# First quad of an attention kernel loaded, transposed and copied one head of each pair at a time, with a rewritten instruction order

## Chip, cores, metric

One core of a Trainium2 chip. The metric is the device time of one execution in microseconds, as the median of several runs; lower is better. In the profile PE is TensorE, PEld its weight load, DVE VectorE, ACT ScalarE, POOL GpSimd and SP SyncE.

## What is computed

Thresholded attention over 8 batches of 8 heads, 576 positions and head size 64, all in float32, followed by a feed-forward layer with a maximum over three projections:

```python
scores = scale * np.matmul(q, k.transpose(0, 1, 3, 2))
thresh = np.max(scores, axis=-1, keepdims=True) - tau          # tau = 0.02
scores = np.where(scores >= thresh, scores, -1000000000.0)
attn = np.exp(scores - max); attn = attn / (sum + 1e-09)
x = (attn @ v) as [4608, 512]
h = np.maximum(np.maximum(x @ w1, x @ w2), x @ w3)              # [4608, 768]
out = h @ w_out                                                # [4608, 512]
```

## The kernel before

Four heads of a batch make a quad; there are 16. A quad holds two pairs of heads; in the code r is the pair and i the head within it. q and k of a quad lie in tiles `qm` and `km` of 128 partitions: head i of each pair is in partitions 64i to 64i + 63, and the two pairs lie beside each other in a partition, each as nine row blocks of 64 numbers. In `transposed`, TensorE turns them with float32 transposes of 64 partitions, head by head, into a PSUM bank (`tp`); `evacuated` copies the bank into `qt` (on ScalarE, which also scales) or `kt` (on VectorE). Of `qt` there is a second copy, `qs`, whose upper and lower 64 partitions are exchanged (`swapped`), so that both row halves of TensorE can work on a score tile at once.

Work goes on in chunks of 128 query rows; a quad has nine, and a chunk has two halves r, one for each pair. Each of the 288 chunk halves runs through one score bank S (`scores`), a maximum m on VectorE, exponents e on ScalarE, and numerators with their sum. The mask list `MASKED` says for each chunk half which way is taken: a 1 lets VectorE apply the threshold after an exponential (letter k, `scalar_tensor_tensor`), a 0 lets ScalarE do it with two activation passes (letter n). After that come a reciprocal r, the normalised bf16 tile P on GpSimd (letter p), a transposing DMA t into `ptq`, the product with v (O, `product`), and the FFN of a whole batch (F and B: the two row halves of a `ph` or `po` piece; h, v, u evacuate them). Letter T is a transposition of a later quad, with a and c for its evacuation and q for its `qs` copies. Letters l and g are loads of q, k, v and of weights, y and z their casts on GpSimd, and o a store.

Nothing is scheduled at run time. The string `ORDER` is read letter by letter, and each letter issues one step; a digit after S, T, O or F names one of four PSUM slots of two banks each. The wrapper `_Ordered` keeps the written order on each engine, so each engine works through its instructions in this order and waits where data is missing. Everything of quad 0 is issued before the string begins: twelve warming transposes on TensorE, `load(0, first=True)`, four `transposed` pieces with their evacuations, and the swapped copies. In this first quad only, VectorE makes one half of each `qs` copy and ScalarE the second `kt`. All instructions go through the wrapper, so the profile puts nearly all of them on its line, L89; tiles tell them apart. DMA transfers use eight completion semaphores in turn, in the order of the program, so a transfer waits until the one eight places ahead of it has landed.

Batch 7 is processed in two parts (`SPLIT`), the last of which leaves only a short FFN at the very end.

Of the kernel before, what the change touches and what calls it, by code (L numbers as in the profile page):

```python
# [23 lines left out]
MASKED = """  # L24
101000100110000110011100001010010001100010001000101000010000100000100010
000011110101100001001001001001000001011100101011000110001010010000010011
001010011101100000101100100001001010000110011111000001000100000110000101
001001001101100000110001000100101000001100010011100101110110000001111111
"""
# [8 lines left out]
ORDER = """  # L38
glllllS0lylS1mylyeS2zmlkS3lelmnlT0mS1aS2rmeqS0meqmeS3pnkT1pT0nrcaptemS0yeS1mgS2eympeS3mqtnT1S0mqnS2knrceprmS
1epkepeS3mnyS0rkptemnS2pmnlzmS3erremtpT0empS1eklpaS2kgnS0ptnmeprrmlS1epS3mleS2pmlS0eplmetpmeS1knS3tkernkS2pt  # L40
nmnprmtepmS1eqS0melpmT2ntrmT3pnrcpatekS3pekS2eqnrS1mtnqmS0pemepS3tmeqS2kepT1lnrcnprtmS0nT1pmS3epmgS2atpmeO1k
yermeO0knptrerT3wpnT2wcS1aptmnS3pS2xmptS1emzS0emeS3zgmeS2lrmpnS0lmO1eplmeplknO3qlnrwleplwkS1xqgS2ertmF3npF0m
eT1pBrteBkyhS2cpnS3mpS1nvF2npmF0eqBmeqBrrvepS3tkhT2pS1nmS0lapmetS2pmeS3mzeF0mF1ezgBrnF2vpgnBktByeF0rvhpS3ntS
2pmF1npmBeBqrveT3zncT0F2taqvS3nBpmnS0tprhS1rmpeS3mtpS2emeyS0mteF1zmeF3kBelqBnvgF2pngT0vBnqlrS1cphS3lrmnS0plm
O2eplmeptS1ewpS3nmF0znmS2lBezkgO3etymyS1vegkF0ntF2wnrrmpBxBpveS3phS0mtnF1prmeBprS2evptS3nmF0pnS1mplBermS3ztn
S2vnzS1meS0tmpeF3mperkS2petBmepmS0tkuF1ukelkT3elBkntrarmpS2uS3pmulS0eymtO1empnrO2kpewS3xpwS1elmpF2lmF0eyqBrl
keT3ytBhcF1pnT2vT3qlaBclnS0qvlS2nqtF3mnyF1meS0pBemBthrrF2kpeS3vnBpmF0nS1pveBrprS3mhtS2pmeS0pmeS1tpmF2emF3peB
tkeT0BvaF1onvqT2T0tBcqaS3nkqS0lhrmS2nlpmF1elpF3meBlkBelF0vntS2rvnBpS1mhplS3melF0mS2teBrmepS1rkpO3emnqO2tnrvp
nwyS0xlprwS3emoF2pmoT1eyBpctS3evyF0nS1mtnS2pmBeympF1hkS3eyF2rekT0ptBamBnpS0veF3qtvS1urmnpS2mF3epketT0nkT1Bnr
mparrcpS2uS1pumtS0empS3emqoS1eF2mqlemqleS3kplnS0mBlepmlekT1teO3kunktO0urcpnrrwlS2nplS1wxmpS3lmpS0eompS1eF2mt  # L50
peF3meBkBetS0khF1nrmF2pnBvpBerrvS3phS0mtnpS1mF2peS3mtpeBmeF1yvF0etByknBvnS2tS3rhmpS1melpS0meF3lmF2elBkeBlvT1
ntF0nvT3BacS2ohS1rrmlpnF3lmF0peoBkpeBovnT2oS1qavS3tnprO2rmpmleqS0wtnT3pS1mepO2mteqkeqF0nS1cxBywmpnS3rS2hytmS
1emF0peF3mpeBrkBpetF2vnF1pBnvS0thkS3nmF2BmeBveF0rrvpT1uS3kapS0nmS2F1pmtepmeS3rktepS0mnS2pmlBelrmeplS3kupS0lu
rmS2elpF1mnoqmeS0qreS2lmpS3elmBpelmptekO0nketO2ukurrnwpT3T1xwpcS0aF2ymyT3tpS1ceBqmS3thqF0meF2pknBtBnvF1nS3rt
rvpeBmS0phS2lmepS1lmyS3etF0meyF2mpeBkBetF1knF3vnBBrvhpS0nvT1pF2nmF3takBeS0rvplBmS1phlrS2remplF3mpleF0klBpeS1
lvnS2lpmnBtrO3mepvnptS2nwS1emF0mF3eBrkepS2hBrmS1nptvS0npT2meO3qmeycqlT0xT1wyS2lacF3ntmyT0yeF1kqBatrBrevqF0hk
S2pnoS3mF1pmBteBpveS2qntS0vpnF3mprS1mlueS3pmoS0nqmtF2epmekT1oBerocpetrkS3npS1nmS0lpumS3uopmS1eT2mF0aokeorS3r
emplS2emtpS1emBpeklqtkO3uqunO0rtmpewpT2wxtS3cpeS0mnF2tF1meBknF3lkBhlBevF2nS0vnBmS1hrrS3pmeF0pmS2eBpmteF1pveF
3kBlnS0vnlS2rrBnmlpS1hrlmpF0eF3mtpeBkpBevtS2nF1pvnT0pBtmaS3hS0metF1rmepT2BrcepS3nvptT0S2nmyS1amS3lepmS0leO2m
lelmeO1rkpewnT3pwF0xcF2nykBnS1vnBrmS3phF0rrmepS2BynmqF1levF3qlBekpF0onvS2tBqmBhqrS1lepvT2S3lampF0lmS2peoBkpe  # L60
tF1vnS3prmuS0ntqmS1eF2pmetpmeS3rkepS1tBmnpmelrS0keptS3muS1uymS0temT2yeF3pcntknT2BkelramtpS1nS2pmuS0leqrmO1tu
qrkepO3nwepmS1xpwS2metF3pmS0eqBmeF1yhrkT2pBtecF3nS0vpnlS2rmpS1nlmBpnF0lveS2tmF3eBmeBkleF1klhF2lnrBvplS0nrrvp
tBnS3mphS1myteS2mF3epmF0eBpeBtvpT1nrS2yvnlS3maF0omnqS1kBepF3temS2hpBrrmeS0ptveS1pmS3nptS2meO0pmeymnqlO3weoke
oF1wxkT0tT2S3rcapBnmlF2pnS0vqtBerrmpS1hF3mqeT2BpncF0evptF2nkBpT1nvBlaS3ylS0hmoF1yqmT2eoBqrcnF0tpS3ervT2pBmaF
1ytkqS2uvnS3qmS1epF0mepmeS2kteT3BrnrcponmpS1uryS3umtS2emF0pepomeS1opnS2mtpeO3myektnO1wnkS2xrS3rewpmS1mpBekpt
eS2muS3purmF1epF0tmeBpkS3ntBhS2rnmpO1empO3xvS2xtnkS1eF3rmpF0emByepBveF1tkS2hS3mBmF0eF2rvepBBpvS1htkO3nmO0xkS
2xeS3rmF0pF1mepBeBtvS2F3vF0mF1kBeBkhF2nrvBpnBrvpS3hS0ptmS1pmeS2mtnF0mF3eBrnpBvnF1pS2vntS0rmpBmF3phoS2eS0omeF
1tmBeBkO2vO0rvpF3kpF1uketeF3kekBwrrkpBukxpuF2F0hptF1vF2pvF0hF1tvF2rvpF0hF1vpF2vF0thF1uvF2uvF0hoF3vF1vF2hoF0v
oO3oO1wovF2xF3uoF0F1hF2vF0vF1hF2vF0vF1hF2vF0vF1hF2vF0vF1hF2vF0vF1hF2vBvF0uuooBF1uuouoo
"""  # L70
# [30 lines left out]
def kernel(  # L101
# [79 lines left out]
    def load(g, first=False):  # L181
        b, qd = quads[g]
        L = Ls[g] = dict(b=b, qd=qd, first=first)
# [516 lines left out]
```

## Time and profile before

| | |
|---|---|
| median of 3 runs | 452.37 us (450.96 to 452.71) |
| the profiled execution's own time | 451.11 us |
| its span on the core | 449.3 us |
| TensorE busy | 425.6 us (95%) |
| VectorE busy | 402.0 us (89%) |
| ScalarE busy | 392.3 us (87%) |
| GpSimd busy | 314.8 us (70%) |
| P on GpSimd | 288 instructions, mean 811 ns |
| loads of 512 KB of q (15 of them) | median 4.9 us from issue to landing |

The span is what the profiler saw from the first to the last instruction of the core; the execution's own time is 1.8 us longer. Busy time of TensorE is an upper reading, since matmuls are pipelined and their ends modelled. All lines of the profile come from this one execution, so they are compared with its 451.11 us and not with the median.

### The profile page before, as it was taken

Reading aid. Unit: us, or ns where it says so; the run is one execution under the profiler, and the core shown is the slowest. Engines: PE = TensorE matmul, PEld = TensorE weight load, DVE = VectorE, ACT = ScalarE, POOL = GpSimd, SP = SyncE. Lnnn points to the kernel's source line nnn. Section 1 sums busy time; section 2 is a strip of 40 time slices with the busy share of each in tenths; the row PEclk is TensorE's granted clock in tenths of the full one; section 3 lists DMA queues with packets and bytes.
Section 4 is the critical chain, followed back from the end, with each engine's and each line's share of the span. In section 5 each row is a group of like instructions: output and inputs, shape, how many; then the busy total and the mean of one; then the engine's idle time right before and its main releaser. Section 6 shows DMA issues by size and latency. Waiting matters only on the chain.

```text
span 449.3 us, 14063 instructions
## 1 busy us (share of the span) xinstructions
PE 425.6 (95%) x5188; PEld 314.8 (70%) x5188; DVE 402.0 (89%) x1115; ACT 392.3 (87%) x794; POOL 314.8 (70%) x416
## 2 busy tenths in 40 slices
PE   6766889999999999999999999999999999999995
PEld 6433557767688768878677867868787787787762
DVE  3999999998999999999989999999999999999541
ACT  3999999999899999999989999999999999866422
POOL 3798889989795985586776785659777787534400
PEclk8989999999999999999999999999999999999999
DMA  8989999999999999996999998999999999546622
GB/s 236 276 208 204 223 214 226 222 231 222 246 212 193 214 221 231 192 222 132 221 166 194 236 217 182 215 229 216 200 172 186 213 175 191 107 77 133 130 94 107
DMA packets 212773, 87.44 MB, mean 195 GB/s; under 512 B 185824, under 2 KB 199648, under 8 KB 212704
## 3 DMA queue, kind: packets, MB, share of 16 engines
q1 hardware_dynamic: 212144, 85.95, 93.4%
q8 instruction: 41, 0.67, 0.6%
q10 hardware_dynamic: 560, 0.59, 0.5%
q14 instruction: 28, 0.23, 0.2%
HBM read 34.60 MB, written 9.44 MB: 98 GB/s over the span
## 4 chain that ended last, share of the span: by engine, by line
PE 75%; DVE 6%; POOL 5%; DMA 5%; ACT 3%; issue 3%; SPq 1%; ACTq 0%; POOLq 0%; DVEq 0%
PE ph L89 30%; PE sc L89 26%; PE po L89 8%; PE o L89 8%; POOL P L89 3%; PE tp L89 3%; DVE z L89 3%; DVE unused L89 2%; ACT z L89 2%; DMA ptq<-P 1%; SPq L89 1%; DMA qm<-in_q_dram 1%; DMA km<-in_k_dram 1%; POOL qs L89 1%; ACT ob L89 1%
## 5 line engine op out<-in xcount | busy, mean ns | idle before, releaser
L89 POOL TENSOR_SCALAR P<-z,rs 128x576 bf16<-128x576 f32 x288 | 229.2, 811 | 89.4 <-DVE rs L89 40.6
L89 PE MATMUL sc<-kt,qs 64*128 64x256 f32 (+2 forms) x640 | 180.2, 421 | 9.2 <-ACT qt L89 3.2
L89 PE MATMUL sc<-kt,qt 64*128 64x320 f32 (+2 forms) x640 | 181.2, 432 | 4.0 <-DVE kt L89 1.2
L89 PE MATMUL ph<-xt,w 64*128 64x288 bf16 (+2 forms) x2160 | 165.0, 283 | 0.3 <-DVE hm L89 0.2
L89 PEld LDWEIGHTS <-w 64*128 64x128 bf16 (+1 forms) x2160 | 127.1, 94 | 29.4 <-issue 6.7
L89 ACT ACTIVATE z<-sc,nm 128x576 f32<-128x576 f32 x179 | 128.8, 742 | 11.6 <-DVE unused L89 9.7
L89 DVE TENSOR_SCALAR_CACHE_REDUCE unused<-sc 128x576 bf16<-128x576 f32 x179 | 130.3, 751 | 4.0 <-PE sc L89 3.4
L89 ACT ACTIVATE z<-z 128x576 f32<-128x576 f32 x179 | 121.0, 682 | 0.1
L89 PEld LDWEIGHTS sc<-kt,qs 64*128 64x128 f32 (+1 forms) x640 | 91.5, 178 | 33.3 <-ACT z L89 7.8
L89 PEld LDWEIGHTS sc<-kt,qt 64*128 64x128 f32 (+1 forms) x640 | 91.6, 177 | 21.0 <-ACT z L89 6.5
L89 DVE SCALAR_TENSOR_TENSOR z<-z 128x576 f32<-128x576 f32 x109 | 89.9, 839 | 0.3 <-ACT z L89 0.2
L89 DVE TENSOR_SCALAR_CACHE_REDUCE z<-sc 128x576 f32<-128x576 f32 x109 | 80.6, 752 | 7.4 <-PE sc L89 3.6
L89 ACT ACTIVATE z<-z,nm 128x576 f32<-128x576 f32 x109 | 81.8, 774 | 4.0 <-DVE z L89 3.4
L89 POOL COPY qs<-qt 64x640 f32<-64x640 f32 (+1 forms) x62 | 45.4, 733 | 14.7 <-ACT qt L89 11.6
L89 PE MATMUL po<-wo,hT 64*128 64x512 bf16 (+1 forms) x480 | 54.0, 356 | 0.1
L89 DVE TENSOR_TENSOR hm<-ph,hm 128x576 bf16<-128x576 f32 (+2 forms) x54 | 37.1, 687 | 12.1 <-PE ph L89 11.6
L89 ACT ACTIVATE hm<-ph 128x576 bf16<-128x576 f32 (+2 forms) x54 | 32.1, 595 | 14.9 <-PE ph L89 14.4
L89 PEld LDWEIGHTS <-hT 64*128 64x128 bf16 (+1 forms) x480 | 29.6, 97 | 16.7 <-issue 3.1
L89 DVE TENSOR_TENSOR hT<-ph,hm 128x576 bf16<-128x576 f32 (+2 forms) x54 | 37.2, 688 | 2.8
L89 PE MATMUL o<-ptq,vb 128*64 128x64 bf16 (+2 forms) x544 | 38.9, 281 | 0.2
L89 ACT ACTIVATION_READ_ACCUMULATOR z<-z 128x1 f32 x179 | 35.7, 199 | 0.0
L89 PEld LDWEIGHTS <-vb 128*64 128x64 bf16 x544 | 23.7, 111 | 14.2 <-issue 4.6
(32 smaller groups left out, 273.8 us busy)
## 6 DMA issues: line engine op xcount, KB each, us to landing
vm<-in_v_dram SPq DMA_DIRECT2D x32, 256.0 KB, 4.5
out_dram<-ob SPq DMA_DIRECT2D x32, 256.0 KB, 2.8
qm<-in_q_dram SPq DMA_DIRECT2D x15, 512.0 KB, 4.9
km<-in_k_dram SPq DMA_DIRECT2D x15, 512.0 KB, 4.7
stage<-in_moe_w_dram SPq DMA_DIRECT2D x9, 512.0 KB, 4.6
ptq<-P SPq DMA_TRANSPOSE x144, 4.1
stage<-in_moe_w_out_dram SPq DMA_DIRECT2D x3, 512.0 KB, 5.8
qm<-in_q_dram SPq DMA_DIRECT2D x16, 64.0 KB, 3.1
```

The lines of the kernel that those rows point to most:

```text
L89: ins = fn(*a, **kw)
```

## The change

The first quad is handled one head of each pair at a time. `load(0, first=True)` now issues, for i = 0 and then i = 1, loads of 64 partitions: q and k of the first head pair with nine row blocks, the tenth block (all 128 partitions, once) and the other pair. There are ten transfers of q and k instead of six; three of them are still on ScalarE's queue, and seven instead of three on SyncE's, ahead of v. Before the string begins only the i = 0 halves are transposed, evacuated and swapped; the i = 1 halves become T, a, c and q steps in the string. In all of quad 0, GpSimd makes every swapped copy, in halves of one head, and VectorE every `kt` copy. There are 14 warming transposes instead of 12, and two more after each `k` transposition (`FILL`). The three banks are used in turn (`x % 3`), because the warming one stays in use.

```diff
-WARM = 12
+WARM = 14
+FILL = (2, 2)
...
         if first:
-            for n, src, e in srcs:
-                e.dma_start(out=L[n][:, 0:8], in_=rows_of(src)[:, 0, 0:8])
-        for n, src, e in srcs:
-            e.dma_start(out=L[n][:, 8:10], in_=rows_of(src)[:, :, 8])
-            yield
-        for n, src, e in srcs:
-            if first:
-                e.dma_start(out=L[n][:, 10:18], in_=rows_of(src)[:, 1, 0:8])
...
+            for i in range(2):
+                rows = slice(64 * i, 64 * i + 64)
+                srcs = (("q", q, sync), ("k", k, sync if i else nc.scalar))
+                for n, src, e in srcs:
+                    e.dma_start(out=L[n][rows, 0:9], in_=rows_of(src)[rows, 0, 0:9])
+                if i == 0:
+                    for n, src, e in srcs:
+                        e.dma_start(out=L[n][:, 9:10], in_=rows_of(src)[:, 1, 8:9])
+                for n, src, e in srcs:
+                    e.dma_start(out=L[n][rows, 10:18], in_=rows_of(src)[rows, 1, 0:8])
...
-        elif L["first"] and r == 1:
-            scalar.activation(out=dst(L["kt"]), in_=src, func=AF.Copy)
         else:
             vector.tensor_copy(out=dst(L["kt"]), in_=src)
-    def swapped(L, r):
+    def swapped(L, r, ii=(0, 1)):
...
-        for x in range(2):
-            e = vector if x == 1 and L["first"] else pool
-            e.tensor_copy(out=L["qs"][64 * x:64 * x + 64, :, cols],
-                             in_=L["qt"][64 - 64 * x:128 - 64 * x, :, cols])
+        for x in (0, 1) if len(ii) == 2 else (1, 0):
+            pool.tensor_copy(out=L["qs"][64 * x:64 * x + 64, ii[0]:ii[-1] + 1, cols],
+                             in_=L["qt"][64 - 64 * x:128 - 64 * x, ii[0]:ii[-1] + 1, cols])
             yield
...
-        p = transposed(Ls[0], n, r)
-        p.first(x)
+        p = transposed(Ls[0], n, r, (0,))
+        p.first(x % 3)
         p.done[0]()
-        if n == "q":
-            for _ in swapped(Ls[0], r):
-                pass
+        if n == "k":
+            for _ in range(FILL[r]):
+                tensor.transpose(warm[:, 0:128], identf, identf)
+    for _ in zip(*(swapped(Ls[0], r, (0,)) for r in range(2))):
+        pass
...
-                T=((g, n, r) for g in range(1, NQ) for r in range(2) for n in "qk"),
+                T=((g, n, r) for g in range(NQ) for r in range(2) for n in "qk"),
...
-            p = transposed(Ls[g], n, r)
+            ii = (0, 1) if g else (1,)
+            p = transposed(Ls[g], n, r, ii)
```

The string `ORDER` is new throughout; each line of it differs. Its first steps were and are:

```diff
-glllllS0lylS1mylyeS2zmlkS3lelmnlT0mS1aS2rmeqS0meqmeS3pnkT1pT0nrcaptem...
+gllS0llS1mlT2lemzT3lkeS0gynlcT1amT3ayS2yecqrqT1mpS0aS3kqeS1mpeS2nmeqt...
```

In both, the first transposition of quad 1 (T0 before, the second T1 after) comes when four scores have been issued. After the last score, both strings end with the same eighteen F pieces of batch 7's first part, the last two products, and the second part's eighteen pieces; before these eighteen the old string has three FFN halves, two products, the short ninth output piece and four output halves, the new one only two output halves; it has the others ahead of its last score.

`MASKED` has 108 ones instead of 109. Counted by 36 chunk halves they were 14, 9, 13, 15, 14, 13, 12 and 19, and are 13, 9, 11, 15, 14, 13, 12 and 21.

More of the change, by code (lines that the diff above doesn't have):

```diff
@@ L24 @@
 MASKED = """
[L25 to L28, printed above, removed]
-"""
-WARM = 12
+101000100110000010011100001010010001100010001000101000010000100000101000
+000011101001100001000001001001000001011100101001100110001010010000010011
+000010110111000100101100100001001010000100111110010001000100000110000101
+001001001101100000110001000100101000001100110011100100111011001111010111
+"""
+WARM = 14
+FILL = (2, 2)
 SLOTS = 4
@@ L44 @@
[L44 to L48, printed above, removed]
@@ L69 @@
[L69 removed]
+gllS0llS1mlT2lemzT3lkeS0gynlcT1amT3ayS2yecqrqT1mpS0aS3kqeS1mpS2nmeqtqmeS0qrmnT1lpS3nclyelrmS1epmeS2mptnS3mpS
+0eT1kytekzanrmS1lempeS2mpeT3rkqtnS0cnpmS3nlqrelrmpeS1lmpnS0lmS2pelpmelpnmtS3erkpS0etmnS2pmnktS1errempT3gekpt
+ekS0nptS2amnprmS3eqmetqS1rmepT2ekpT0nS3mnpmtS1aprcnS0plmeS2lpmetyremS3qeS0mpT1gempteS2cqeS3knS1kS0nrnprmnpmT
+2tepmT3epmatrkpeS2cnS1tzmeS3rnmO0pnkqteO1meprwlnS2pwS0xmpteS1mpeS3mzelS2rknT1lS0palmeO1qtmeymnO3rlkeylnwT2pl
@@ new lines @@
+ncgS1pxrgrS2wpmetF3pnmS0S1epmBeymF0qntkF2phBeBvpF3eS0vqnBrktnpS1T2mhpamtS3ezrS2rmeS0lmpeS1mpeF2gmF3peBnyF0vn
+BkzS2eBvnS1mhF3ygymnpF0tBrerpBevtpS2nF1vpnT3mBpnT0cS2tqarmS3epS0hmtzeS1mzeS2mteF3mpnF0rktpBeBevF1qnlS2vqnBrm
+pT3ngS0cplS2hrmS3npgmO1lepmleqS2welpS0remS1pnmO3zemegkF2zxtF0wkeBnF3pgBvntBrnrvS1pS2hrmpF0mS3peBmpetF1vpeS2p
+S0nmlBnzmS3eS2rvlzeS0tmS1npmF3npmtermpS0eBmpetkeF2ektukT1uS0knBlrnmpaS3pleS0myS1ulrrukO3lynmopeO2mleqwleyS0p
+wlxS3lmpnF1tmF2qeBkpeT0tBhcF3yrT1vT0aByrcnS2tqvF1nqS0mnpS3tmeF2pmBeylBkphF0nvS1lpeBmF2tvS3eBrrmnpS0lhS1pmleS
@@ new lines @@
+2pmleS3pmtF1emF0eBketT2BrvapF3nT2vtqT1nBcpnS0rtpS2amhpS1meF0tqmF3eBrkeptBvnF2pS1nvoBynmS0hS3tmyeF1qmS2eqlBme
+S0lrnrvO3lpnkpnO1mepwteS2pwrrxS3mptnF0mT1peBcpS3elvF2nplS1mnS0lmBelrmS1eptF3mepF0knBtT1hkBarF2vpetS1vpuS3rmp
+S2tF0mepmetT1knT2BknocaS3urrS2pumoS1epmlS0emqtS2eF3mpempleS1klqeS2lmT0nBtqmekeO1knrnkpO2nrcpwS0xpwtuS1muS2pm
+eS3qtrmF1epS0meF2pomeBkBeS3lkhF0tnmF1nBrvpBerrS2vphS3mpntS0mF1peS2myetBpmnF0pvF3elBrkepBlnvS1lS2phmlS0meS3tm
+eF2mF1etBkeBvT0nF3nvT2BarcS1phS0rmpnF2mpF3teBkpeT1BvaS0nrtvS1pnmO2pnomeorS3wpeT1lS0mqntO2mqerkqelF3cxlS0nprw
@@ new lines @@
+oS1mnqBomS2eptS0mhpF1emF3pteBkyBevF2nF0vpnBkS1ythS3rmyF2pmBepBveF1trnvpS0urpT3nmS2yatS1meS0myF3eplrmepkS1ept
+S2nmS0pmBelqmelkS2elS1kuF0ourrmpS3ompeS2ompeBlmpelkeS1lkO3ulnktnO2rmpuwntqT1wT0xrpcS3aF2ymepT1BtceqS0khS1pF3
+tnmF2nqrrBmetpBvF1epS0vnpBtmS3phS2metS1mS0eF3melF2meBkBelF1knF0vBBrvhpS3nvF1pnF2mtT0kBaS3rvepBrmS0phS1meptF2
+mpeF3kBelS0vnlBmnS1orO2melprnvlqS0nlwpS1lemF3plF2rmeqtBkpeS0BhmtS1npvS3npT0mO2eymecT3xtT1wrS0acpF2emqT3tF1kq
+eBrBkapS0hS3vnF1pmtnF2ymBeyByrveS0nvpF1nmptS3uS2rpemS1pmtF0emperT3ktepS2nBmpnocqS1turS2pumS3emplT0nS1mqtaS2k
@@ new lines @@
+F3ermepmS0epS1emtBekekS2lumO0nlkelO1wnlrrulmpT0xlS3wcpeS1mqF0tF2mpeBkyeBkF3hpF1nrvBnqtS0vnBprmS2hpS3meF0ptmS
+1epBmeyF2tkeF3BvnlS1rnvpBlnS0mplS2hmF1temF3eBrkplBevF0nlT2prvS1npBtamS3phrS2mepF0tmepT1rBecpS3tnvqT2nS1mqS0a
+mpS3emS2yteO1rmeqmnlpO0wleplF1wxtkT3nF0ceBlkBnS3rvhpS2mnF1pS0rmeyBqmeF2pvF3eyBkynlBrvF1lhS0rnpoBmT2pS3vaoyS0
+mpeF1ompS2eoBkpetS3mnF0qvntS2rumS1peF0myetpmeS3knS1trmBepmeplrkS2eqoS3umlS1upmT2ntS0pmeF3metrceT0pBeklaklS1u
+qlS2umS0tqnmO3pnkleO1trrempnwpS2xwS3pmeF1pmS0etBrkepF2mhT3BnylcF1nvS3ynprlS2meBytmpS3evF0pnS2mteF1mBekBleF3r
@@ new lines @@
+khpF2tnBvS0pnrrvBlnpS1mlhS3ymelS2mtpF1emF0peBktepBT3vnS2ratvpS1nmF3pnS0moBermF1peoS2rqhBtmepS3veS0pmlS1nplS2
+mntO3mekeO1lmeoweF0twrxkT3pT2S1caBpnmF2nqS3vBeqrmtS0hpF1meT2pBncoF3qnvF2ekBtT1nrvS0paBrrmpS3hF1ymteqT2BceqS0
+nvF3pnF2kpmBuT1ptvS2aS0pmeS3qtmF1eqrmepT2oeS3cpBnktnmS0urS2rulmpS3emlpF1emptekS0pnS3mnO2mtekeO0rerwpS3wxpkS2
+pS0tBmpmelymetyS3kuS0yuF2emF1BrmepBkhyS3eS2vpnO0mtnO1kxS3xrmeS0pF1epmF2rtmBepBvepS3hS1tmnF0kF2nBkeF3mBBrvepS
+1hvpO0mO3txrS2xpeS0mpoF3mF1eBkoeBkonF0F2tvnBkF3hvBnBrvpS0rF1vpS2mptBrS3mpeS0mhptS2empF1emF3tekBBvF2okF0oBkF1
@@ L70 @@
+hkBeBvnF2vO3uvO0wrrS2xpS1mpS3mF0eptmepkF1noekS2tBmkeBukuorrF3pF2hpF0vF3pvtF2hF0pvF3rvpF2thF0vpF3vF2thF0vF3vF
+2hoF0vF3vF2hF0uvuO3oF2owvO1uoF3xF0F2hF1vF0vF2hF1vF0vF2hF1vF0vF2hF1vF0vF2hF1vF0vF2hF1vBvF0uuooBF2uuouoo
 """
@@ L182, in load @@
         b, qd = quads[g]
-        L = Ls[g] = dict(b=b, qd=qd, first=first)
+        L = Ls[g] = dict(b=b, qd=qd)
         for n in "qk":
@@ L189, in rows_of @@
             return src[b, 4 * qd:4 * qd + 4].rearrange("(r i) (p c) d -> (i p) r c d", r=2, c=9)
-        q2 = nc.scalar if first else sync
-        srcs = (("q", q, sync), ("k", k, q2))
         if first:
-            for n, src, e in srcs:
-                e.dma_start(out=L[n][:, 0:8], in_=rows_of(src)[:, 0, 0:8])
-        for n, src, e in srcs:
-            e.dma_start(out=L[n][:, 8:10], in_=rows_of(src)[:, :, 8])
-            yield
-        for n, src, e in srcs:
-            if first:
-                e.dma_start(out=L[n][:, 10:18], in_=rows_of(src)[:, 1, 0:8])
-            else:
-                e.dma_start(out=L[n].rearrange("p (r c) d -> p r c d", r=2)[:, :, 0:8], in_=rows_of(src)[:, :, 0:8])
-            yield
+            for i in range(2):
[8 more added lines that the diff above has]
+                    e.dma_start(out=L[n][rows, 10:18], in_=rows_of(src)[rows, 1, 0:8])
+        else:
+            for n, src in (("q", q), ("k", k)):
+                sync.dma_start(out=L[n][:, 8:10], in_=rows_of(src)[:, :, 8])
+                yield
+            for n, src in (("q", q), ("k", k)):
+                sync.dma_start(out=L[n].rearrange("p (r c) d -> p r c d", r=2)[:, :, 0:8], in_=rows_of(src)[:, :, 0:8])
+                yield
         L["vm"] = ld.tile([128, 4, 4, D], F32, name="vm")
@@ L255, in targets, with transposed @@
                 L["qs"] = qk.tile([128, 2, S], F32, name="qs")
-    def transposed(L, n, r):
+    def transposed(L, n, r, ii=(0, 1)):
         st = {}
@@ L266, in first @@
             for j in range(nj):
-                for i in (1, 0):
+                for i in ii[::-1]:
                     rows = slice(64 * i, 64 * i + 64)
@@ L274, in done @@
             off = 320 * r
-            evacuated(L, n, r, lambda t: t[:, :, off:off + 64 * nj],
-                      st["ps"].rearrange("p (i z) -> p i z", i=2)[:, :, 0:64 * nj])
+            evacuated(L, n, r, lambda t: t[:, ii[0]:ii[-1] + 1, off:off + 64 * nj],
+                      st["ps"].rearrange("p (i z) -> p i z", i=2)[:, ii[0]:ii[-1] + 1, 0:64 * nj])
         return _Piece((L["b"], L["qd"], n, r), first, None, [done])
@@ L645, in issue @@
         elif what in "ac":
-            p, g, r = line[what].pop(0)
+            p, g, r, ii = line[what].pop(0)
             p.done[0]()
             if what == "a":
-                line["q"].append((Ls[g], r))
+                line["q"].append((Ls[g], r, ii))
         elif what in "hvuxw":
```

27 lines of the change are left out of this document (1 added, 26 removed).

## The prediction

> **What bounds the kernel now.** I read the totals of the page first, then busy time by stretch, then the timeline and the chain of the first 15 us, which is where the change is made, and last the stretches of the end.
>
> The totals (engine, busy us, share of the span, instructions):
>
> ```profile
> PE 425.6 (95%) x5188; PEld 314.8 (70%) x5188; DVE 402.0 (89%) x1115; ACT 392.3 (87%) x794; POOL 314.8 (70%) x416
> ```
>
> Busy time by stretch. The columns are the stretch, its length, PE, PEld, DVE, ACT and POOL busy, granted clock, DMA share, GB/s:
>
> ```profile
> 10.00:20.00 10.00, 7.14 (x74) 4.73 (x71) 9.48 (x26) 8.50 (x16) 6.82 (x11) 0.93 0.95 301
> 20.00:30.00 10.00, 8.08 (x56) 4.25 (x54) 9.66 (x31) 9.98 (x23) 8.87 (x13) 0.83 0.89 184
> 30.00:40.00 10.00, 6.14 (x46) 2.88 (x44) 9.44 (x31) 9.94 (x20) 8.43 (x10) 1.00 0.99 195
> 40.00:50.00 10.00, 6.71 (x58) 3.73 (x58) 9.67 (x30) 10.00 (x22) 9.44 (x13) 1.00 1.02 216
> ```
>
> From 20 to 50 us ScalarE has nothing to spare, VectorE little, GpSimd 1 us in 10 and TensorE 2 to 4. So before the FFN has input, the softmax engines set the pace, and an earlier first score helps only if these three engines also keep their lead after it. The end is different:
>
> ```profile
> 430.00:440.00 10.00, 10.00 (x76) 6.91 (x76) 5.77 (x12) 2.63 (x6) 0.00 (x0) 1.00 0.04 11
> ```
>
> There TensorE alone runs. The start, from the timeline (start, length, instruction, idle before it):
>
> ```profile
> 5.17 0.64 PE L89 MATMUL tp<-identf,qm 64*128 64x64 f32 x10 [0.99 <-DMA qm<-in_q_dram]
> 5.86 0.70 ACT L89 ACTIVATE qt<-tp 128x640 f32<-128x640 f32 x1 [2.42 <-PE tp L89]
> 6.59 0.49 DVE L89 COPY qs<-qt 64x640 f32<-64x640 f32 x1 [4.86 <-ACT qt L89]
> ...
> 6.88 0.47 PE L89 MATMUL tp<-identf,qm 64*128 64x64 f32 x8 [0.75 <-DMA qm<-in_q_dram]
> 7.11 0.82 DVE L89 COPY kt<-tp 128x640 f32<-128x640 f32 x1
> 8.08 0.76 PE L89 MATMUL sc<-kt,qs 64*128 64x256 f32 x1 [0.48 <-ACT qt L89]
> 9.56 0.76 DVE L89 TENSOR_SCALAR_CACHE_REDUCE z<-sc 128x576 f32<-128x576 f32 x1 [1.12 <-PE sc L89]
> 14.39 0.76 DVE L89 TENSOR_SCALAR_CACHE_REDUCE unused<-sc 128x576 bf16<-128x576 f32 x1 [0.33 <-PE sc L89]
> ```
>
> The first score waits until 8.08, the first maximum until 9.56. The chain of waits shows what comes next:
>
> ```profile
> 4.93 0.62 SPq L89
> 5.60 0.61 SPq L89
> 6.25 0.59 SPq L89
> ...
> 7.96 5.14 DMA qm<-in_q_dram
> ...
> 13.23 0.53 PE tp L89 x10
> ```
>
> SyncE issues one transfer after another, quad 1's q is issued at 7.96 and lands at 13.10, its transpose follows at 13.23, and the scores queued behind that transpose on TensorE come after it. So the second bound of the start is the load of quad 1, not quad 0.
>
> **The head start.** The first two load stages of quad 0 (512 KB, then 640 KB) release TensorE at 5.17 and 6.88: 1.71 us for 640 KB. The first stage now has 218 KB less, so it lands 0.58 earlier, about 4.6; at the other end no earlier. Then five transposes (half of 0.64), one scaled copy of 320 columns (0.70 for 640 and 0.60 for 512 make 0.45), one GpSimd half copy (0.74 for 640 and 0.63 for 512, from the two pairs after 14 us, make 0.47 for 320), beside them the four kt and qt halves and, for bank 0, the evacuation of the second kt. With 0.1 us between engines the first score starts near 6.6 instead of 8.08 and the first maximum near 7.2 instead of 9.56: at most 2.4 us won, with no less than 1.0 if the loads land no earlier and the clock is half.
>
> [...]
>
> **What moves off and on.** VectorE loses two qs copies (0.49 + 0.42) and gains the second kt as two halves, while its first kt is split: about 0.45 + 0.40 twice, 1.70 against 0.82, so +0.88. One masked half fewer (109 to 108 ones) takes 0.84 off. Net about -0.9. ScalarE loses the 0.59 of kt, pays 0.40 for splitting two qt copies, and gains one exponent pass with sum, 0.68: net +0.5. GpSimd makes eight half copies (four of 0.47, four of 0.41, 3.5) where it made two (0.95 + 0.87): +1.7. TensorE gets two more warm transposes and four fillers of 0.21 each, all before the first score and beside waits for data: nothing, or 0.4 if they delay the first score.
>
> **Where the head start goes.** SyncE has seven loads ahead of v instead of three. The program uses eight DMA completion semaphores in turn, so the ninth transfer waits for the first to land; that is the wait before the v remainder at 4.93 above. In the changed order the ninth is the upper half of q, and it, the upper half of k and both vm issues now stand behind that wait. From the issue rows: 4.93 - 0.58 = 4.35, plus 0.52 + 0.52 + 0.80 + 0.68 for these four, plus the unchanged 3.03 from the v remainder to q of quad 1, makes 9.9 where it was 7.96. The weight stage that GpSimd casts first moves by the same 1.9. Landings move between 0 (the DMA engines were backed up anyway) and 1.9 (they follow the issue). I take 1.5, nearer the second, because SyncE's waits and not bytes set the spacing.
>
> That gives, at the first transpose of quad 1, which stands after only four scores in both orders:
> VectorE reaches its fifth maximum at 14.39 + 1.5 = 15.9. It has by then done one masked numerator and both kt upper halves more (7.2 us of work before, 8.0 after), so 393.1 of its 401.1 are left against 394.8 of 402.0. It stands at 15.9 + 393.1 against 14.39 + 394.8: 0.2 earlier.
> ScalarE copies quad 1's first qt at 13.80 + 1.5 = 15.3; behind it 386.7 of 392.8 are left against 386.8 of 392.3: 1.4 later.
> GpSimd casts the weights first now, at 10.97 + 1.5 = 12.5; v, four half copies, quad 1's qs, four P, the next v and the second qs pair, 12.0 us together by their rows, end at 24.5. Before, the P that follows these started at 23.03: 1.5 later.
> ScalarE and GpSimd are the engines without room from 20 to 50, so I take their 1.4 to 1.5 and not VectorE's 0.2.
>
> [...]
>
> A first score at full clock takes 0.3 less; the later ones are paced by the 0.84 of a maximum, so the clock is worth 0.3 once, inside the head start.
>
> **The rest of the order.** Counted off the two texts with the rows' means (score half 0.49, FFN half 0.49, output half 1.30), TensorE has the same work behind it at every twelfth score within 1.1 us up to score 276, save one place (2.3). In the last twelve, the new order brings 6.7 us of FFN and product work ahead of the last score. TensorE runs without pause there in both, so this moves work and costs nothing, with a bound of +1.5: the last transposed P landed at 425.78 and its product started at 425.94, so nothing covers a later P. The sum against the profiled execution: 451.11 (span 449.3 and 1.8 around it) + 1.5 = 452.6. The median of the runs, 452.37, is 1.26 above that execution; put on the median, 453.9.
>
> **The rivals.** [...]
> *The head start is kept.* DMA was already full (0.95 from 10 to 20), so quad 1 still lands near 13.1. VectorE is then 1.7 ahead, ScalarE and GpSimd level, so 452.4 at most, and 449.7 if the whole 2.4 and the clock's 0.3 reach the end. Against it: SyncE's wait at 4.93, with more behind it.
> *The new order itself is better.* The chain of before passes through waits on landings and evacuations at 164 to 170, 216 to 226 and 100 to 112, some 25 us of chain that is not TensorE's. If the new order saves a tenth to a fifth of it net of the late start: 447.4 to 449.9. For it speaks that these waits are not bound by work; against it, that the new order has the same work per score, so no more cover.
>
> **How the numbers follow.** Forecast (head start lost to quad 1's load, 452.5 to 455.3): 0.42. Half-rate loads: 0.25. Head start kept: 0.18. Better order: 0.15. About 0.5% (2.3 us, so 450.1 and 454.6) is what a measurement of this kernel can tell from no change. Faster: all of the better order and 0.07 of the kept head start, 0.22. Slower: the half-rate case and 0.12 of the forecast, 0.37. Within: 0.41. The range leaves out most of the better order (0.13) and the top of the slow case (0.07): 449.8 to 457.
>
> **What would show it.** First score at 6.3 to 7.0; q of quad 1 issued at 9.5 to 10.3 and landed at 14 to 15; VectorE and ScalarE idle for over 1.5 us between 13 and 16; the fifth maximum near 15.9. I am wrong if quad 1's first transpose comes before 13.5, if the P of quad 0 come no later than before, or if the tail of TensorE opens gaps ahead of the last products.

## The result, and the profile after

The changed kernel took 456.97 us (median of 4 runs, 456.28 to 458.45) against 452.54 for the kernel before in the same comparison (4 runs): ratio 1.0120, 95% interval 1.0096 to 1.0143. It is slower by 4.4 us by the medians and 5.4 by the ratio; the forecast was 453.9, so 3.1 less. 456.97 lies just inside the stated range (449.8 to 457), at the end that was put there for half-rate loads. The profiled execution took 457.2 us, with a span of 455.4.

Totals of the page of the changed kernel:

```profile
PE 434.3 (95%) x5194; PEld 321.2 (71%) x5194; DVE 401.4 (88%) x1114; ACT 392.5 (86%) x797; POOL 312.9 (69%) x422
```

Work is what it was; VectorE, ScalarE and GpSimd are busy within 2 us of before. Of TensorE's 8.7 us more, 4.5 lie in the first 50 us, where it ran fewer matmuls (270 against 286) at a lower granted clock (0.87 instead of 0.94 from 10 to 50 us), and 6.0 behind 400 us, where the longer kernel is still at work. So these totals do not tell waits from slow matmuls. By stretch, columns as before:

```profile
10.00:20.00 10.00, 8.39 (x57) 6.98 (x55) 6.88 (x20) 6.60 (x13) 6.06 (x10) 0.83 0.90 283
20.00:30.00 10.00, 7.20 (x70) 3.61 (x66) 9.86 (x27) 8.81 (x18) 9.01 (x13) 1.00 0.85 165
30.00:40.00 10.00, 8.88 (x46) 6.12 (x46) 8.93 (x29) 10.00 (x24) 7.47 (x10) 0.66 0.94 210
40.00:50.00 10.00, 6.54 (x60) 3.40 (x60) 8.84 (x28) 9.67 (x21) 9.77 (x12) 1.00 1.18 185
430.00:440.00 10.00, 10.00 (x116) 7.46 (x115) 4.13 (x10) 3.76 (x9) 0.00 (x0) 1.00 0.42 122
```

Between 10 and 20 us VectorE is busy 6.88 instead of 9.48 and ScalarE 6.60 instead of 8.50. The start on the timeline:

```profile
4.54 0.69 PE L90 MATMUL tp<-identf,qm 64*128 64x64 f32 x4
...
6.68 0.69 PE L90 MATMUL warm<-identf 128*128 128x128 f32 x2
...
8.34 0.69 PE L90 MATMUL warm<-identf 128*128 128x128 f32 x2
...
9.02 0.76 PE L90 MATMUL sc<-kt,qs 64*128 64x256 f32 x1
...
10.50 0.76 DVE L90 TENSOR_SCALAR_CACHE_REDUCE z<-sc 128x576 f32<-128x576 f32 x1 [1.62 <-PE sc L90]
...
18.03 0.76 DVE L90 TENSOR_SCALAR_CACHE_REDUCE unused<-sc 128x576 bf16<-128x576 f32 x1 [1.64 <-PE sc L90]
```

The first transposes are early (4.54 instead of 5.17), the first score is late (9.02 instead of 8.08), and the fifth maximum is 3.6 late (18.03 instead of 14.39). The chain of waits shows what the fifth waits for:

```profile
8.68 0.51 SPq L90
...
9.23 0.47 SPq L90
...
9.74 6.32 DMA qm<-in_q_dram
...
16.20 0.62 PE tp L90 x10
```

SyncE issues q of quad 1 at 9.74 (7.96 before), and it now needs 6.32 us to land (5.14 before), until 16.06.

How much of this belongs to the change is seen from the experiments' kernels, whose starts repeat each other (their names are explained below):

| | first score | fifth maximum | q of quad 1 landed |
|---|---|---|---|
| ten narrow loads (changed kernel, e3, e6, y1, y4) | 7.80 to 9.02 | 16.92 to 18.19 | 14.97 to 16.06 |
| six wide loads, otherwise changed (e1, e5, e7, e8, y3) | 7.76 to 9.09 | 14.51 to 17.27 | 12.27 to 13.37 |
| first quad of before (before, e2, all x, y2) | 7.81 to 8.48 | 14.19 to 15.86 | 12.44 to 13.72 |

The late landing belongs to the change. The late first score does not: its spread is the same with either loads.

**A measure for the middle.** From about 80 us on TensorE hardly pauses (before, it is busy for 319.2 of the 320 us to 400), so what counts is how much of its work is still to do. Busy time does not show it: from 280 to 340 us the changed kernel's TensorE is busy for 59.6 of 60 us and yet gets through 754 matmuls where before has 774. I take every matmul not yet begun at a time, with the mean start-to-start time of its tile between 280 and 400 us in the kernel before (ph 63 ns, sc 120, tp 36, o 64, po 100), and subtract the same sum for before. This is microseconds of TensorE work that a kernel is behind; the experiments are in it already (split orders are explained below):

| behind before at (us) | 20 | 40 | 60 | 80 | 160 | 280 | 340 | 400 |
|---|---|---|---|---|---|---|---|---|
| changed kernel | 3.2 | 2.9 | 3.8 | 4.4 | 5.1 | 3.8 | 5.8 | 6.0 |
| e1: with wide loads | -0.2 | 0.5 | 0.3 | 3.7 | 4.2 | 3.1 | 5.2 | 5.3 |
| e2: old start, new order | 1.9 | 1.4 | 2.9 | 3.1 | 3.5 | 3.1 | 5.2 | 5.3 |
| y1: new start, old order from score 32 | 1.7 | 2.4 | 2.1 | 4.5 | 4.5 | 3.8 | 4.1 | 4.1 |
| y3: y1 with wide loads | 0.5 | 1.4 | 1.4 | 1.6 | 2.6 | 2.2 | 2.2 | 2.1 |
| x5: new order to score 32, then old | 0.0 | 0.5 | 0.1 | 0.4 | 0.6 | 0.5 | 0.7 | 0.5 |
| x2: new order to score 82, then old | 0.5 | 1.2 | 1.4 | 1.5 | 1.6 | 1.6 | 1.7 | 1.6 |
| x1: old order to score 82, then new | 0.0 | 0.0 | 0.0 | -0.3 | 0.6 | 0.1 | 2.1 | 2.2 |
| y2: x1 with five letters moved | -0.5 | 0.0 | 0.2 | 0.3 | 2.2 | 2.0 | 2.7 | 3.0 |
| y4: changed kernel, same five moved | 1.9 | 2.0 | 2.6 | 2.8 | 3.4 | 2.7 | 3.6 | 3.8 |

A single execution is uncertain by some 2 us in this table: x1 and y2 issue the same steps until 190 scores, and y2 falls back by 1.8 between 100 and 120 us where x1 falls back by 0.2; x8, which has before's steps until score 244, is 2.2 behind at 280. Only what many kernels repeat is used. One loss lies ahead of 80 us. The other lies between 280 and 340: 1.9 to 2.2 us in all eleven kernels that have the new order there as it is (the changed one, e1 to e8, x1, x3), and at most 0.4 in the six with the old order there (x2, x5, x8, x9, y1, y3).

### The profile page after: what moved, and what is told of

It reads as the page before. It is cut to its first block, busy times and chain, and to the rows that moved or that the text cites. A ratio compares the mean times of both kernels' runs of the same rounds, so it can differ in the third digit from the quotient of the medians.

```text
span 455.4 us, 14104 instructions
## 1 busy us (share of the span) xinstructions
PE 434.3 (95%) x5194; PEld 321.2 (71%) x5194; DVE 401.4 (88%) x1114; ACT 392.5 (86%) x797; POOL 312.9 (69%) x422
## 4 chain that ended last, share of the span: by engine, by line
PE 81%; DVE 4%; issue 3%; POOL 3%; DMA 3%; ACT 3%; SPq 2%; ACTq 0%; POOLq 0%; DVEq 0%
PE ph L90 30%; PE sc L90 29%; PE po L90 10%; PE o L90 9%; PE tp L90 3%; POOL P L90 3%; ACT z L90 2%; SPq L90 2%; DVE z L90 1%; DMA qm<-in_q_dram 1%; DVE unused L90 1%; DMA ptq<-P 1%; DVE kt L90 1%; POOL qs L90 1%; DMA km<-in_k_dram 0%
## 5 line engine op out<-in xcount | busy, mean ns | idle before, releaser
L90 POOL TENSOR_SCALAR P<-z,rs 128x576 bf16<-128x576 f32 x288 | 223.3, 788 | 98.6 <-DVE rs L90 44.8
L90 PE MATMUL sc<-kt,qt 64*128 64x320 f32 (+2 forms) x640 | 187.2, 439 | 4.8 <-ACT z L90 2.8
L90 PE MATMUL sc<-kt,qs 64*128 64x256 f32 (+2 forms) x640 | 185.9, 428 | 5.3 <-ACT z L90 1.3
L90 PEld LDWEIGHTS sc<-kt,qs 64*128 64x128 f32 (+1 forms) x640 | 93.0, 181 | 29.3 <-ACT z L90 7.5
L90 PEld LDWEIGHTS sc<-kt,qt 64*128 64x128 f32 (+1 forms) x640 | 93.0, 181 | 21.6 <-ACT z L90 6.7
L90 POOL COPY qs<-qt 64x640 f32<-64x640 f32 (+3 forms) x68 | 47.7, 703 | 11.4 <-ACT qt L90 7.8
L90 PEld LDWEIGHTS <-hT 64*128 64x128 bf16 (+1 forms) x480 | 32.1, 97 | 15.2 <-issue 2.9
L90 PEld LDWEIGHTS <-vb 128*64 128x64 bf16 x544 | 22.0, 111 | 17.2 <-issue 7.6
```

The costliest lines, as they stand in the source:

```text
L90: ins = fn(*a, **kw)
```

## Experiments

Times are given as ratio to the kernel before with its interval; 0.001 is 0.45 us. "New order" is the new string with its new mask; where it follows the old start, the twelve quad-0 steps (T, a, c, q) are taken out.

**The new first quad, its parts.** e1 gives the changed kernel the six wide loads of before (the diff shows one of each); e4 keeps ten transfers of nearly the same sizes on the same queues but lets each cover all 128 partitions with about half the row blocks (c0 is blocks 0 to 4, then 5 to 8); e3 takes the fillers out.

```diff
 e1
-e.dma_start(out=L[n][rows, 0:9], in_=rows_of(src)[rows, 0, 0:9])
+e.dma_start(out=L[n][:, 0:8], in_=rows_of(src)[:, 0, 0:8])
 e4
-e.dma_start(out=L[n][rows, 0:9], in_=rows_of(src)[rows, 0, 0:9])
+e.dma_start(out=L[n][:, c0[0]:c0[1]], in_=rows_of(src)[:, 0, c0[0]:c0[1]])
 e3
-WARM = 14
-FILL = (2, 2)
+WARM = 12
+FILL = (0, 0)
```

> The changed kernel, with the six 128-partition loads of quad 0 from before; halves, GpSimd copies, fillers and order stay changed. Theory A (the narrow loads run at about 200 GB/s where wide ones ran at 350, so everything behind them lands some 3 us later): quad 1's q lands near 13 us instead of 16.06, the first score starts by 8.3 instead of 9.02, total 452 to 454, so 3 to 5 of the 4.4 us lost come back. Theory B (seven issues on SyncE and the wait for the first landing set the pace): the same here, since the issues go too. Theory C (the new order or the GpSimd copies cost the time): stays at 455.5 or more.

> The changed kernel with ten transfers of the same sizes in the same order on the same queues, but each over all 128 partitions and half the row blocks, so that a first half of the bytes is no longer one head of each pair and the first transposes wait for more transfers. Theory A (narrow loads are slow): the transfers land 0.6 us apart as SyncE issues them, quad 0 is complete before 8 us instead of 8.69, quad 1's q lands by 14.5 instead of 16.06, first score 8.7 to 9.5, total 454 to 455.5. Theory B (issues and completion waits): quad 1's q still lands near 16, total 456.5 or more.

> The changed kernel without the four filler transposes and with 12 warm ones. Theory D (the fillers stand in the way: the second pair's transposes waited from 6.7 to 7.3 behind two of them): first score 0.4 to 0.7 us earlier, total 456.2 to 456.7 against 456.97. Theory A: the quad 1 load sets the pace and the total stays within 0.4 us. If the fillers did their work, the first scores run at half clock as they do now, because the clock is 0.50 there anyway.

Measured: e1 1.0119 (1.0088 to 1.0149), e4 1.0104 (1.0073 to 1.0135), e3 1.0122 (1.0099 to 1.0144). The total does not move. At the start, quad 1's q landed at 12.64 in e1 (issued at 7.46), at 16.05 in e3 (10.03), and at 15.41 in e4, 6.08 us after its issue:

```profile
9.33 0.47 SPq L90 DMA_DIRECT2D qm<-in_q_dram  x1
...
15.55 0.53 PE L90 MATMUL tp<-identf,qm 64*128 64x64 f32 x10 [0.39 <-DMA qm<-in_q_dram]
```

Full width has quad 0 itself complete at 7.61, where the five kernels with narrow loads have 8.41 to 9.09. But quad 1's q then lands at 15.41, within their 14.97 to 16.06, and only six transfers instead of ten bring it back to 12.64. So its late landing goes with the number of transfers for the most part. The first scores, 7.76 in e1 and 8.03 in e3, lie within the spread shown above and say nothing on loads or fillers. e1 is only 0.3 behind at 60 us and 3.7 at 80.

**The new order alone.** e2 is the kernel before with its own first quad, and the new string and mask.

> The kernel of before with its own first quad, but with the new order string and mask (the steps for the second half of quad 0 taken out of the string). Theories A and B: the order is worth little, total 451.5 to 453.5 against 452.5 of before. Theory C (the new order itself costs the time): 455 to 457.

Measured: 1.0105 (1.0077 to 1.0134), 4.7 us. The order by itself costs nearly what the whole change costs.

**Where in the order.** The strings were cut at the same number of issued scores and joined; at the seam up to seven letters are evened out, slots are renamed, and the mask changes four halves ahead of the cut.

```diff
-ORDER = old
+ORDER = new[:218 steps] + old[218:]      # x5, cut at score 32
+ORDER = old[:218] + new[218:]            # x3, cut at score 32
+ORDER = new[:406] + old[406:]            # x9, cut at score 54
+ORDER = new[:652] + old[653:]            # x2, cut at score 82
+ORDER = old[:653] + new[652:]            # x1, cut at score 82
+ORDER = old[:2202] + new[2205:]          # x8, cut at score 244
```

> The new order and mask until 32 scores, the old ones from there, with before's start. If the loss lies in the stretch from score 32 to 82: 452 to 453.5. If it lies in the first 32 scores: 455.5 to 457.

> The old order and mask until 32 scores, the new ones from there, with before's start. If the loss lies in the stretch from score 32 to 82, where the products of the second quad wait for the last turned probabilities: 455.5 to 457.5. If it lies in the first 32 scores: 452 to 454.

> The mirror of the kernel before this one: before's start, the new order and mask until 82 scores, the old ones from there. Theory A (loss ahead of score 48): 455 to 457.5. Theory B (loss behind it): 452 to 453.5.

> The kernel before, whole, with its own order and mask until 82 of its 288 scores have been issued, and the new order and mask from there (one transposition step is evened out at the seam; slots renamed). Theory A (the loss arises in the new order ahead of score 48, where the second quad's products wait for its turned probabilities): 452 to 454. Theory B (the loss arises behind that, in the middle of the new order): 455 to 458. The traces of e1 and e2 put about 1.5 us behind maximum 48, so 453.5 by theory A with that.

> Before's start, the new order and mask until 54 scores, the old ones from there. Until 32 the new order cost nothing (451.63), until 82 it cost 2.1 (453.79). If the 2.1 arise where the first products stand among the scores of quad 2 (scores 40 to 50, 50 to 62 us): 453 to 454.5. If they arise behind score 54: 451.3 to 452.3.

> Before's start, order and mask until 244 scores, the new ones from there. In the traces of every kernel with the new middle TensorE falls 2 us behind between 280 and 340 us (scores 196 to 240), and not behind it. If that reading is right, 451.5 to 452.5, so that the splice at 82 (454.84) owes its loss to that stretch. If the loss of the splice at 82 lies in the new tail: 453.5 to 455.

Measured: x5 0.9997 (0.9979 to 1.0016); x3 1.0107 (1.0084 to 1.0130); x9 1.0033 (1.0017 to 1.0049); x2 1.0046 (1.0030 to 1.0063); x1 1.0067 (1.0044 to 1.0089). So the new order costs nothing up to score 32, 2.1 us up to 82 and 3.0 behind it, and the sum, 5.1, is e2's 4.7. Of the 2.1, 1.5 are there at score 54 (the intervals of x9 and x2 overlap). Theory A of x1 and x2 (all of it ahead of 48) and theory B (all of it behind) both fall: it is in two places. x8 came out at 1.0057 (1.0030 to 1.0084), 454.10 us, which by its own expectation speaks for a loss in the new tail. Its profile loses nothing from 280 to 340 us, as expected, but 1.5 from 340 to 360, just behind its cut, where one masked numerator takes 1.58 us (0.76 before, 0.81 in x1). x1, which has the new steps there without a cut, loses nothing from 340 to 400, nor does any other kernel with the new tail lose over 0.3. I take the loss of x8 for one of its seam; that is argued, not shown.

**The first place.** In e1 TensorE falls back when it waits for the transposed P of quad 1's last chunk (timeline of e1, of the changed kernel, and of before, in turn: the second quad's products):

```profile
65.76 1.39 PE L90 MATMUL o<-ptq,vb 128*64 128x512 bf16 x14 [2.02 <-DMA ptq<-P]
```

```profile
68.49 1.12 PE L90 MATMUL o<-ptq,vb 128*64 128x512 bf16 x14 [0.75 <-DMA ptq<-P]
```

```profile
63.02 1.20 PE L89 MATMUL o<-ptq,vb 128*64 128x512 bf16 x15
```

Before, nothing is waited for. In the new string a weight cast (z) and a qs copy (q) stand ahead of the last two P of that quad on GpSimd, and a 256 KB load of v (l) ahead of their transposing DMA on SyncE. e7 moves only l, e8 only z and q, e5 all three, each in e1; e6 all three in the changed kernel.

```diff
-...S1tzmeS3rnmO0pnkqteO1meprwlnS2pwS0xmpteS1m...
+...S1tmeS3rnmO0pnkteO1meprwnS2pwS0xmpzqtleS1m...
```

> The wide-load version with only the v load moved behind the last transposed P of quad 1. Theory G: its transfer takes 3.3 instead of 4.6 us, so it lands 1.2 earlier, total 456 to 456.6 against 457.44. Theory H: no change within 0.5.

> The wide-load version with only the weight cast and the qs copy moved behind that P on GpSimd. Theory G: P comes 1.0 to 1.7 earlier, total 455.8 to 456.5 against 457.44. Theory H: no change within 0.5, or slower if the cast or the copy is late for who needs it.

> The wide-load version of the new order (457.44), with three steps moved a few letters back in the string, so that the last P of quad 1 and its transposing transfer go first: the weight cast and one qs copy on GpSimd now come after that P, and the load of v on SyncE after that transfer. Theory G (a gate: quad 1's products wait near 64 us for that transposed P, which landed at 65.6 here and 63.0 in the kernel of before): it lands by 64, the 2.0 us gap of TensorE before the products closes, VectorE's lag at 70 us falls from 4.1 to 2 or less, total 454 to 455.5. Theory H (the new order loses the time in many places, and the gate only shows it): 456.5 or more.

> The changed kernel as it is, with the same three steps moved back. Theory G plus a late start: VectorE is already 4.2 us behind at 40 us, so the gate adds little there and the move brings at most 1.5: 455.5 to 457. If the gate alone cost the time: 453 to 454.5.

Measured: e7 1.0064 (1.0022 to 1.0106), e8 1.0084 (1.0064 to 1.0104), e5 1.0096 (1.0070 to 1.0121), e6 1.0095 (1.0074 to 1.0117). All are lower than what they start from (1.0119 and 1.0120), by 2.5, 1.6, 1.0 and 1.1 us, but every interval overlaps it, and all three moves together give no more than one. In all four traces the wait for that P is gone (under 0.1 us), and they are still 2.8 to 4.0 us behind at 80 us. e2, e3, x2 and x3 have these letters unmoved, show no such wait either, and are 3.1, 4.3, 1.4 and 2.7 behind; y1, with the old order there, waits 0.93 us for a transposed P at 67.4. So this wait is not what is lost here; e1 is one execution in which it was long.

The granted clock of TensorE is a rival that no run here separates. In e1 it was 0.50 from 66.5 to 69.9 us, just behind the wait, and there a product of 512 columns took 615 ns where before takes 384; this is part of the 3.4 us that e1 loses from 60 to 80. Such stretches at half clock, 3.4 to 6.9 us long, lie between 51 and 61 us in e2, x2, x3 and x9, while before, x1 and x5 have none between 43 and 400. Against it, x8 and y2 have one of 3.4 us between 49 and 55 and are only 0.8 and 0.3 behind at 80. Whether waits lower the clock there or the clock makes the loss is not shown. The cuts show where the first place is, behind score 32 and mostly ahead of 54; what it is stays open.

**The new first quad in the old order.** y1 is the changed kernel with its own order until 32 scores and the old one behind; y3 is the same with before's six wide loads.

```diff
-ORDER = after
+ORDER = after[:230 steps] + old[218:]     # y1; y3 also has the loads of e1
```

> The changed kernel's first quad (its ten narrow loads, fillers, GpSimd copies) and its own order and mask until 32 scores, the order and mask of before from there. If the loss of the change belongs to the rewritten order behind score 32 and the stretch between 40 and 50 us absorbs a late start: 451 to 453, like the same splice with before's first quad (451.6). If the late start of the new first quad (its first maximum 0.9 late, its fifth 3.6) reaches the end by itself: 454 to 455.5.

> The changed first quad followed by the order of before (as in the splice that gave 455.34), but with before's six loads of 128 partitions for quad 0. If the narrow loads are what makes the new first quad cost 3.3 us: 451.0 to 452.8, at best faster than before by the 0.9 us that the first maximum comes earlier. If the splitting of the work itself (GpSimd copies, twice as many steps, its place in the order) costs it: 454.5 to 456.

Measured: y1 1.0075 (1.0045 to 1.0105), 455.34 us; y3 1.0034 (1.0012 to 1.0056), 453.4 us. x5, the same string with the old first quad, was at 0.9997. My leaning after e2, that the first quad is innocent, falls: by itself it costs 3.4 us, and six wide loads instead of ten narrow ones bring back 1.9 of it (the two intervals overlap a little). y3 changes width and number of the loads together; the landings of e4 speak for the number. What the other 1.5 is was not tried.

**The second place.** The chain of waits from 275 to 345 us, by line, in before, in the changed kernel and in y2:

```profile
by line: PE ph L89 38.7%; PE sc L89 38.1%; PE o L89 9.8%; PE po L89 8.6%; PE tp L89 4.9%
```

```profile
by line: PE sc L90 33.8%; PE ph L90 33.0%; PE o L90 11.1%; PE po L90 10.1%; PE tp L90 3.9%; issue 2.7%; DVE unused L90 1.9%; DVE z L90 1.2%; DVE hm L90 1.0%; ACT xt L90 0.9%; DVE xt L90 0.3%; DVE rs L90 0.2%; DVE hT L90 0.1%; POOLq L90 0.0%
```

```profile
by line: PE sc L89 37.5%; PE ph L89 36.4%; PE po L89 8.5%; PE o L89 7.4%; DVE z L89 3.8%; PE tp L89 3.5%; ACT z L89 2.1%; ACT xt L89 0.9%; ACT ob L89 0.7%; DVE xt L89 0.3%; issue 0.3%
```

Before, TensorE alone carries this stretch, as in x2, x8, x9, y1 and y3. In the new order as it is, the chain leaves TensorE for the issue gaps and VectorE's maxima (2.7% and 1.9% in e2, e3, e6, x1 and x3 too). The timeline there, changed kernel first, then before:

```profile
283.50 0.28 POOL L90 CAST vr<-vr 64x128 bf16<-64x128 f32 x1
...
283.61 1.50 DVE L90 SCALAR_TENSOR_TENSOR z<-z 128x576 f32<-128x576 f32 x1
...
283.77 0.74 POOL L90 TENSOR_SCALAR P<-z,rs 128x576 bf16<-128x576 f32 x1
...
284.57 1.01 POOL L90 COPY qs<-qt 64x512 f32<-64x512 f32 x1
...
285.04 1.15 DVE L90 SCALAR_TENSOR_TENSOR z<-z 128x576 f32<-128x576 f32 x1
```

```profile
273.22 2.10 POOL L89 COPY qs<-qt 64x512 f32<-64x512 f32 x2
...
279.05 0.75 DVE L89 SCALAR_TENSOR_TENSOR z<-z 128x576 f32<-128x576 f32 x1
...
279.73 0.75 DVE L89 SCALAR_TENSOR_TENSOR z<-z 128x576 f32<-128x576 f32 x1
...
283.35 0.75 POOL L89 TENSOR_SCALAR P<-z,rs 128x576 bf16<-128x576 f32 x1 [5.75 <-DVE rs L89]
```

The first masked numerator of each pair of rows belongs to the same chunk half; the second does not, since the masks differ here. Before they take 0.75 each while GpSimd is idle (from 277.60 to 283.35); in the changed kernel 1.50 and 1.15, having begun during a cast that a P follows, and during a qs copy. It goes both ways: in the kernel before, a P that begins during a masked numerator takes 1.26 us on average (35 of them), one that begins first and is met later 0.76 (42), one that meets none 0.75 (211). In the rows above, 1.50 and 1.15 both end 0.6 us behind the GpSimd work that they met (285.11 behind 284.51, 286.19 behind 285.58).

y2 takes x1 and moves two qs copies into GpSimd's idle time some 5 us earlier, a v remainder cast a little later, and, 30 us on, a masked numerator behind the next maximum and a qs copy behind the next P. y4 makes the same moves in the changed kernel. These are five letters; the texts on record speak of six.

```diff
-mO1nlkelO0wnlrrulmpT1xlS3wcpeS0mqF1tF2mpeBkyeBkF3hpF0nrvBnqtS1
+mO1nlkelqqO0wnlrrulmpT1xlS3wcpeS0mF1tF2mpeBkeBkF3hypF0nrvBntS1
...
-eF0ompS2eoBkpetS3mnF1qvntS2rumS0peF1
+eF0ompS2eoBpetS3mknF1vntS2rumS0pqeF1
```

> The splice old until 82, then new (454.84), with six letters moved in the stretch where its TensorE falls behind: two qs copies of GpSimd some 5 us earlier, into its idle time at 272 to 276 us, one v remainder cast a few letters later, one masked numerator of VectorE behind the next maximum, and one qs copy behind the next P. Theory: there VectorE's masked numerators took 1.50, 1.15 and 1.27 us instead of 0.75 because each began while GpSimd was at a P or a qs copy, TensorE waited for the maxima behind them; with the two kept apart 452.8 to 454.0, and the numerators at these places near 0.75. Rival (they are stretched but hide, and TensorE is held by something else): 454.4 to 455.3.

> The changed kernel as it is (456.97), with the same six letters moved between scores 190 and 222 that took 1.3 us off the splice at 82. Theory (masked numerators begun while GpSimd is at a P or a qs copy hold the maxima, and TensorE behind them): 455.3 to 456.0. Rival (that gain came from elsewhere): 456.6 to 457.5.

Measured: y2 1.0037 (1.0018 to 1.0056) against x1's 1.0067 (1.0044 to 1.0089); y4 1.0092 (1.0061 to 1.0124), 456.12 us, against 1.0120 (1.0096 to 1.0143). Each gives about 1.3 us, and each pair of intervals overlaps; but the traces say the same: from 280 to 340 us x1 loses 2.0 and y2 0.7, the changed kernel 2.0 and y4 0.9. The two numerators of the changed kernel's rows came down to 0.76 and 0.75 (y2's timeline), and the third, the moved one, from 1.27 to 0.76. Another, six chunk halves on, went up from 0.89 to 1.24, and one ahead of them from 0.75 to 1.15; TensorE lost less all the same:

```profile
281.36 0.76 DVE L89 SCALAR_TENSOR_TENSOR z<-z 128x576 f32<-128x576 f32 x1
...
282.05 0.75 DVE L89 SCALAR_TENSOR_TENSOR z<-z 128x576 f32<-128x576 f32 x1
```

No kernel of these beats the one before; x5 equals it.

## Why the prediction was wrong

*What failed first: "The rest of the order."* I counted TensorE's work behind every twelfth score, found it equal within 1.1 us save one place, and put the new order at nothing with a bound of +1.5. Alone it costs 4.7 us (e2): nothing up to score 32, 2.1 from there to 82 and 3.0 behind (x5, x2, x1). The count was of work, and where the cause is shown the loss is waits: same work, other neighbours. Between 280 and 340 us, where 2.0 us are lost, masked numerators that begin while GpSimd works (1.50 and 1.15 us instead of 0.75) hold up the maxima behind them, and moving five letters won about 1.3 back. A count of work does not show which numerator meets which GpSimd copy. The rival "the new order itself is better" failed with it: the new order was to save waits, and it brought some into a stretch where before TensorE had none in the chain.

*Second: the size of the late start.* I had added 1.5 us of the 1.9 by which quad 1's q is issued later. It landed at 16.06, not 14 to 15, 3.0 later than before, and the fifth maximum came at 18.03 instead of 15.9; in the four other kernels with these loads it landed at 14.97 to 16.05. The issue itself, 9.74 where I had 9.9, came out right for another reason than mine: SyncE did not wait for the first landing, but issued back to back from 0.73 on (with these loads in y1 and e3 it did wait, and came to 9.95 and 10.03). The narrow issues on SyncE took 0.49 to 0.60 us each, where the wide ones of e4 took 0.33 to 0.43.

No run shows the half rate of the case to which the forecast gave 0.25. What the runs show: the 131 and 147 KB blocks of quad 0 landed 0.51 to 0.73 us apart, some 200 to 290 GB/s, where before's second stage moved 640 KB in 1.71, 383 GB/s. But SyncE also issued these blocks 0.54 to 0.64 us apart, so the rows cannot tell rate from issue. e4 can: with ten transfers over all 128 partitions quad 0 is complete 1.1 us earlier than in the changed kernel, but quad 1's q lands only 0.65 earlier, within the spread of the narrow loads. So issue, not bytes, spaces them for the larger part. With the old order behind it the new first quad gives 455.34, with number and width of the loads both in it; and e1, with wide loads, is no faster than the changed kernel, so slow narrow loads do not explain the measured 457. That the time came out inside the range is luck: the range's upper end stood for them.

*Why the two do not add.* 3.4 and 4.7 would be 8.1; together they are 5.4; with intervals of 1.1 to 1.4 us to each side, the difference is only just clear of noise. My reading, which no run tests, is that lateness up to about 80 us, where TensorE becomes the bound, counts once, whichever of the two brings it: at 80 us the changed kernel is 4.4 behind, y1 4.5, e1 3.7 and e2 3.1. My argument that the three softmax engines carry a lateness to the end saw the stretch from 20 to 50 and not the one behind it.

*The head start.* The first score came at 9.02, not 6.6, and at 7.80 to 8.98 in the other kernels with these loads. The first transposes were early as forecast; but the tenth row block, which the fifth transpose needs and which my sum left out, landed only at 5.81, and on TensorE the first score stands behind the second pair's transposes and two fillers. Fillers were "nothing, or 0.4"; what they cost is not shown, since e3's 8.03 without them lies within that spread, and its total is the same. (The first stage has 224 KB less, not 218; that moves my 0.58 to 0.60.)

*What held:* VectorE's and ScalarE's work hardly changed (-0.6 and +0.2 us; I had -0.9 and +0.5), though GpSimd's fell by 1.9 where I had +1.7; the head start was lost to quad 1's load; and the tail was neutral: from the 277th maximum to the end it is 56.3 us in both kernels, so moving 6.7 us of work ahead of the last score cost nothing.

*What stays open:* what the 2.1 us of the first place are, and the clock's share in them; the 1.5 us of y3; and some 0.7 of the second place.

## What to carry to other kernels

A rewritten static order is not priced by counting work per step, even where it is equal everywhere: look for what stands in each queue just ahead of the item another engine waits for, and if that can't be seen, widen the range by the waits that the whole chain holds. Once one engine is saturated, plot how much of its work is left over time, for both kernels; cutting and joining the two orders then tells in a few runs which stretch loses. Trust in such a plot only what several kernels repeat: here executions of the same steps differed by 2 us, and a wait seen in one trace led me to move letters without a clear gain. And judge a start only together with the first place where the bound changes hands.

## What the hardware showed that I had not expected

A masked numerator that begins while GpSimd works can be stretched from 0.75 up to 2.26 us (behind three P in a row, x1 at 213 us; 2.42 in e1 at 25 us): in the changed kernel 35 of the 50 that begin so take longer than any of the 58 others (0.76), up to 2.26 at 217.5 us. But the one at 213 moved no total that could be seen: x1 is 0.5 behind at 200 us and 0.1 at 280. Such meetings are no more frequent in the new order: 50 of its 108 masked numerators begin during GpSimd work, 63 of 109 before, and the mean length is 0.84 us in both. What was seen to cost time here are those on TensorE's path (y2 won 1.3 us back there).

The clock after the warming transposes is not settled by them. Before had a granted clock of 1.00 from 4.5 to 8.0 us, behind transposes alone, and of 0.50 from there to 11.4, where its first scores ran (64x320 in 0.74 us or more, against 0.53 at 15.85 us, at 1.00); e2 has the same twelve transposes and start and reached lasting full clock only at 19.7 us. In eight of the twenty traces (before, e1, e6, e7, e8, x9, y1, y2) full clock came at 4.3 to 5.5 us, when TensorE had run nothing but transposes, and in the other twelve at 10.1 to 20.3. So transposes alone gave no dependable clock in these runs.
